# The last 128 columns of one matrix product turned round for three tiles of four, in a fused attention and MLP kernel

## The chip, the core and the metric

The kernel runs on one core of a Trainium2 chip. The metric is the device time of one execution in microseconds (us). Before the change the median of three executions is 261.24 us (261.08 to 261.54).

## What is computed

The input `x` has 2048 tokens of 640 values. Two branches read it and a gate mixes them. Of the reference, cut to what matters here:

```python
g = sigmoid((x * gate_w).sum(-1, keepdims=True))
a = linear_attention(x, wqkv, wo)                  # 32 heads of 20
h  = gelu(layernorm(x) @ w1)                       # 640 -> 640
hs = concat([h[:160] one token later, h[160:320] one earlier,
             h[320:480] two later,    h[480:] two earlier]) @ w2
x1 = x + hs
b  = x1 + gelu(layernorm(x1) @ w3) @ w4            # 640 -> 1728 -> 640
out = g * a + (1 - g) * b
```

The change is in the product with `w2` and in the sum `x1 = x + hs` behind it. The second layernorm needs, for each token, the sum and the sum of squares of `x1`.

## The kernel before

Tokens are cut into 16 tiles of 128 (t = 0 to 15) and 4 chunks of 512 (c = 0 to 3); 640 features are 5 slices of 128 (k = 0 to 4). The five engines each run a list of instructions in order, with semaphores between them. TensorE (PE) multiplies into PSUM, which has 8 banks of 512 fp32 columns; VectorE (DVE) and ScalarE (ACT) empty the banks; GpSimd (POOL) normalizes; SyncE (SP) issues nearly all DMAs, among them transposes by the crossbar (`dma_start_transpose`, L285).

The stages around the change:

- **W1** (`w1_group`, L1068): for chunk c and feature block j, 5 matmuls of 512 columns give h with features on partitions; ACT writes the gelu into `hsT` (L1074), shifted by one or two tokens. The block j = 4 takes four gelus, one for each group of 32 features.
- **W2** (`w2_tile`, L1076): for tile t the weights are slices of `hsT` and the moving operand is `w2`: 5 matmuls of 512 columns into one bank and 5 of 128 columns into the bank beside it (`pair()` takes two neighbouring banks). One DVE operation over 640 columns (`stt`, L1081, profile line L657) adds `x_tok` and stores the sum of each token in `st2[:, 0, t]`.
- **SQ** (`w2_sq`, L1083): ACT squares `x_tok` of tile t and stores the sum of squares (profile line L675).
- **S2** (`ln_chunk_stats`, L835): seven small POOL operations per chunk make mean and scale, once its four tiles have both sums.
- **N2 and T2** (`normalize` L853, `t_xn` L859): POOL writes the normalized tile into one of three `xn` buffers, and SP has it transposed into `xnT`.
- **W3** (`w3_group`, L1086): 13 groups of 5 matmuls of 512 columns per chunk read `xnT` of four tiles. `w3_half` (L1095) does the last 64 features of two chunks.
- **QN, QT, AT** (L1113 to L1158): the attention's quotients on DVE, their transposes on SP and its output products on PE.
- **W4** (L1202): the last product. For the first 128 output columns it already works turned: outputs on partitions, 512 tokens moving, then an ACT copy to `tlT`, a crossbar transpose to `tl` (`turn`, L1151) and sums on DVE.

**What sets the order.** Nothing is ordered by hand after the start. `_Items.run` (L352) is a planner in the program that builds the kernel. Every step is an item in a stream, with a duration, dependencies and lags. An item's priority is its duration plus the largest "lag plus priority" of what follows it (in its stream or by a dependency). The planner keeps its own model of when each engine is free. At each step it takes the item with the smallest `max(est, t_pe)`, where `t_pe` is when PE comes free and `est` is when the model has the item's inputs done plus 100 ns; then items of duration 0 (SQ, S2, N2, T2, QN); then the higher priority. Lags count in the priority, not in `est`. The order in which items are taken is the order of instructions on every engine, so an instruction that waits holds back all behind it on its engine. A PSUM bank is chosen in the same pass: `bank()` (L534) takes the one that the model has free first.

W1 and W2 are two streams that the planner interleaves by priority:

```python
IT.add("W1", ("w1", c, j), 1.08, ...)   # L1256
IT.add("W2", ("w2", t), 1.33, ...)      # L1264, needs w1(c, 4) and, for t % 4 == 3, w1(c + 1, 4)
IT.add("SQ", ("sq", t), 0.0, ...)       # L1265, needs w2(t)
```

The buffers `tlT` and `tl` lie in memory that `pk_tok`, the attention's keys, holds earlier (`ra` and `rb`, L473 and L474).

Of the kernel before, what the change touches and what calls it, by code (L numbers as in the profile page):

```python
# [6 lines left out]
F32 = mybir.dt.float32  # L7
ACTF = mybir.ActivationFunctionType
ALU = mybir.AluOpType

S = 2048
D = 640
# [3 lines left out]
NT = S // 128  # L16
NCH = S // 512
KD = D // 128
# [414 lines left out]
def _build(nc, A_x, A_wqkv, A_wo, B_w1, B_w2, B_w3, B_w4, gate_w, out, dbg=None, stop=None):  # L433
    sch = _Sched(nc)
# [37 lines left out]
    pa = Arena(SB_LO, SB_HI - SHARED)  # L472
# [3 lines left out]
    ps = nc.alloc_psum_tensor("ps", [128, 8, 512], F32)  # L476
# [9 lines left out]
    negh = pa.alloc("negh", [128, 4], F32)  # L486
    st1 = pa.alloc("st1", [128, 8, NT], F32)
    st2 = pa.alloc("st2", [128, 8, NT], F32)
    stg = pa.alloc("stg", [128, 4, NT], F32)
    lr = pa.alloc("lr", [128, NT, 2], F32)  # L490
    w3 = pa.alloc("w3", [128, KD, F], BF16)
    w1 = pa.alloc("w1", [128, KD, D], BF16)
    w2 = pa.alloc("w2", [128, KD, D], BF16)
    wo_aug = pa.alloc("wo_aug", [128, 6, D], BF16)
    x_tok = pa.alloc("x_tok", [128, NT, D], BF16)
    xnT = pa.alloc("xnT", [128, KD, S], BF16)
    hsT = pa.alloc("hsT", [128, KD, S + 4], BF16)
# [24 lines left out]
    tlT = rb.alloc("tlT", [128, 3, 512], BF16)  # L522
    tl = rb.alloc("tl", [128, 3, 4, 128], BF16)
# [10 lines left out]
    def bank():  # L534
        best = None
        for k_ in range(nbanks[0]):
            b = (bank_rr[0] + k_) % nbanks[0]
            if b in bank_pend or b in bank_hold:
                continue
            lk = sch.locks.get(b)  # L540
            tfree = 0.0 if lk is None else sch.ev_time.get((lk[1].sem, lk[1].val), 1e18)
            if best is None or tfree < best[0]:
                best = (tfree, b)
        bank_rr[0] = best[1] + 1
        bank_pend.add(best[1])
        return best[1]

    psf = ps[:, :, :].rearrange("p b n -> p (b n)")
    bank_hold = set()

    def pair():
        best = None
        for k_ in range(4):
            q_ = (bank_rr[0] // 2 + k_) % 4
            tf = 0.0
            ok = True
            for b in (2 * q_, 2 * q_ + 1):
                if b in bank_pend or b in bank_hold:
                    ok = False
                lk = sch.locks.get(b)  # L560
                if lk is not None:
                    tf = max(tf, sch.ev_time.get((lk[1].sem, lk[1].val), 1e18))
            if ok and (best is None or tf < best[0]):
                best = (tf, 2 * q_)
        b = best[1]
        bank_rr[0] = b + 2
        bank_pend.update((b, b + 1))
        return b
# [8 lines left out]
    def nfree(ap):  # L577
        n = 1
        for d_ in ap.shape[1:]:
            n *= d_  # L580
        return n

    def in_psum(ap):
        return ap.tensor.name == ps.name

    def act(fn, reads, writes, cost=None):
        if cost is None:
            n = nfree(writes[0])
            cost = max(150.0, 100.0 + 0.833 * n + (70.0 if (reads and in_psum(reads[0])) else 0.0))
            cost += 45.0 * max(0, len(reads) - 1)  # L590
        return sch.op("act", fn, reads, writes, cost=cost)

    def dve(fn, reads, writes, cost=None):
        if cost is None:
            n = nfree(writes[0])
            cost = 65.0 + n / 0.96
        return sch.op("dve", fn, reads, writes, cost=cost)
# [7 lines left out]
    def pe(fn, reads, writes, cost=500.0, after=None):  # L605
        for w_ in writes:
            sp_, rl = sch.rects(w_)
            if sp_ == "ps":
                for (_p0, _p1, lo, hi) in rl:
                    for b in range(lo // PS_BANK, (hi - 1) // PS_BANK + 1):  # L610
                        bank_pend.discard(b)
        return sch.op("pe", fn, reads, writes, cost=cost, after=after)

    def mm_group(out_ap, pairs, reads_extra=()):
        n = len(pairs)

        def fn(e, out_ap=out_ap, pairs=pairs, n=n):
            ins = None
            for i, (l, r) in enumerate(pairs):
                ins = e.matmul(out_ap, l, r, start=(i == 0), stop=(i == n - 1))  # L620
            return ins
        reads = [a for p in pairs for a in p] + list(reads_extra)
        return pe(fn, reads, [out_ap], cost=n * (max(nfree(pairs[0][1]), 24) * 0.4167 + 2.5))
# [28 lines left out]
    def stt(out_ap, in0, scalar, in1, op0, op1, accum=None):  # L652
        rd = [in0, in1] + ([scalar] if not isinstance(scalar, (int, float)) else [])
        n = nfree(out_ap)
        cost = (65.0 + n / 0.96) if (in_psum(in0) or in_psum(in1)) else (160.0 + 1.04 * n)
        if accum is not None:
            return dve(lambda e: e.scalar_tensor_tensor(out_ap, in0, scalar, in1, op0, op1, accum_out=accum), rd,  # L657
                       [out_ap, accum], cost=cost + 70.0)
        return dve(lambda e: e.scalar_tensor_tensor(out_ap, in0, scalar, in1, op0, op1), rd, [out_ap], cost=cost)  # L659
# [3 lines left out]
    def activation(out_ap, in_ap, func, scale=1.0, bias=0.0, accum=None):  # L663
        rd = [in_ap] + [a for a in (scale, bias) if not isinstance(a, (int, float))]
        wr = [out_ap] + ([accum] if accum is not None else [])
        n = nfree(out_ap)
        cost = max(150.0, 100.0 + 0.833 * n + (70.0 if in_psum(in_ap) else 0.0)) + 45.0 * (len(rd) - 1)
        if accum is not None:
            cost += 91.0
        st_ = ACT_SET.get(func)  # L670
        if st_ is not None and st_ != sch.act_func:
            cost += 1290.0
            sch.act_func = st_
        if accum is not None:
            return act(lambda e: e.activation(out_ap, in_ap, func, bias=bias, scale=scale, accum_out=accum), rd, wr, cost=cost)  # L675
        return act(lambda e: e.activation(out_ap, in_ap, func, bias=bias, scale=scale), rd, wr, cost=cost)  # L676
# [91 lines left out]
    IT = _Items()  # L768
# [66 lines left out]
    def ln_chunk_stats(st, c, rs):  # L835
        cs = slice(4 * c, 4 * c + 4)
        ts(pool, st[:, 2, cs], rs, 1.0 / D, 0.0, ALU.mult, ALU.add)
        ts(pool, st[:, 3, cs], st[:, 1, cs], 1.0 / D, EPS_LN, ALU.mult, ALU.add)
        tt(pool, st[:, 4, cs], st[:, 2, cs], st[:, 2, cs], ALU.mult)
        tt(pool, st[:, 5, cs], st[:, 3, cs], st[:, 4, cs], ALU.subtract)  # L840
        tt(pool, st[:, 6, cs], st[:, 5, cs], negh[:, 0:4], ALU.pow)
        tt(pool, st[:, 7, cs], st[:, 2, cs], st[:, 6, cs], ALU.mult)
        ts(pool, st[:, 7, cs], st[:, 7, cs], -1.0, 0.0, ALU.mult, ALU.add)
# [224 lines left out]
    def w1_group(c, j):  # L1068
# [3 lines left out]
        for (p0, p1, sh) in PIECES[j]:  # L1072
            o0 = 2 + 512 * c + sh
            activation(hsT[p0:p1, j, o0:o0 + 512], ps[p0:p1, b, :], ACTF.Gelu_apprx_tanh)  # L1074

    def w2_tile(t):  # L1076
        tok = slice(2 + 128 * t, 2 + 128 * (t + 1))
        b = pair()
        mm_group(ps[:, b, 0:512], [(hsT[:, k, tok], w2[:, k, 0:512]) for k in range(KD)])
        mm_group(ps[:, b + 1, 0:128], [(hsT[:, k, tok], w2[:, k, 512:D]) for k in range(KD)])  # L1080
        stt(x_tok[:, t, :], psf[:, 512 * b:512 * b + D], 1.0, x_tok[:, t, :], ALU.mult, ALU.add, accum=st2[:, 0, t:t + 1])  # L1081

    def w2_sq(t):  # L1083
        activation(junk[:, 0, :], x_tok[:, t, :], ACTF.Square, accum=st2[:, 1, t:t + 1])
# [163 lines left out]
    for c in range(NCH):  # L1248
        for j in range(KD):
            deps = [(("t1", u), 0.9) for u in range(4 * c, 4 * c + 4)] if j == 0 else []  # L1250
# [6 lines left out]
    for t in range(NT):  # L1257
        c = t // 4
        deps = [(("w1", c, KD - 1), GEL)]
        if t % 4 == 3 and c + 1 < NCH:  # L1260
            deps.append((("w1", c + 1, KD - 1), GEL))
        if t == 0:
            deps.append((("g", KD - 1), 0.0))
        IT.add("W2", ("w2", t), 1.33, lambda t=t: w2_tile(t), deps)  # L1264
        IT.add("SQ", ("sq", t), 0.0, lambda t=t: w2_sq(t), [(("w2", t), 1.0)])  # L1265
        if t % 4 == 3:
            IT.add("S2", ("s2", c), 0.0, lambda c=c: ln_chunk_stats(st2, c, st2[:, 0, 4 * c:4 * c + 4]), [(("sq", t), 1.0)])
    for u in range(NT):
        deps = [(("s2", u // 4), 3.2 + 0.9 * (u % 4))]
# [8 lines left out]
    for c in range(NCH):  # L1278
        for j in range(KFF):
            deps = []  # L1280
# [4 lines left out]
            if j == 0:  # L1285
                deps = deps0 + [(("t2", u), 0.9) for u in range(4 * c, 4 * c + 4)]
# [11 lines left out]
    for t in range(NT):  # L1298
        deps = [(("zb",), 1.0), (("q", max(t, 3)), 2.0)]
        if t < 7:  # L1300
            i = (5 * t) // 2 + 3
            deps.append((("w1", i // KD, i % KD), 0.0))
        else:
            i = 3 * (t - 7)
# [7 lines left out]
    for t in range(NT):  # L1312
        c = t // 4
        deps = [(("qt", t), 3.0), (("w4load",), 0.0), (("mq",), 1.0), (("mt",), 2.5)]
# [72 lines left out]
```

## Time and profile before

| | |
|---|---|
| median of three executions | 261.24 us |
| the profiled execution | 261.42 us |
| its span, first to last instruction | 259.7 us |
| PE busy | 255.9 us (99%) |
| DVE busy | 154.4 us (59%) |
| ACT busy | 111.6 us (43%) |
| POOL busy | 98.5 us (38%) |
| granted TensorE clock | 1.000 |

The profiled execution is 1.7 us longer than its span, which does not contain start and end of the program. Times in the trace count from the first instruction. PE stands for matmuls and PEld for the weight loads that run beside them. A matmul's listed duration (379 ns for 512 columns) is its latency; matmuls overlap, so what one costs is the distance from its start to the next one's start. In a timeline row the first number is the start, the second the time that the merged instructions took together, and brackets at the end hold the idle time before and what ended it. A line number in a row is often that of a helper: L620 is every matmul of `mm_group`, L676 every `activation` without a sum, L642 and L659 the DVE or POOL helpers `ts` and `stt`.

### The profile page before, as it was taken

How to read it: one execution, taken by the hardware profiler on the slowest of the kernel's cores; microseconds unless marked ns; L12 is line 12 of the kernel's file. 1: busy time of each engine (PE TensorE's matmuls, PEld its weight loads, DVE VectorE, ACT ScalarE, POOL GpSimd, SP SyncE). 2: the span in 40 equal slices, each digit the busy share in tenths (PEclk: the TensorE clock that was granted, in tenths of full speed). 3: DMA queues.
4: the chain of work that ended last, by engine and by line, in shares of the span. 5: the costliest groups of instructions: out<-in, count | busy, mean ns of one | idle time of the engine just before them, and what ended most of it. 6: DMA issues, size and time to landing. Idle time of an engine off the chain costs nothing.

```text
span 259.7 us, 3906 instructions
## 1 busy us (share of the span) xinstructions
PE 255.9 (99%) x1474; PEld 124.5 (48%) x1474; DVE 154.4 (59%) x286; ACT 111.6 (43%) x226; POOL 98.5 (38%) x154
## 2 busy tenths in 40 slices
PE   7999999999999999999999999999999999999996
PEld 3555555554445554555444444444444444444443
DVE  2497787889912799979995303998006510049136
ACT  1486767751355756694774240015510055200100
POOL 8103996869965018867663210111002210003000
PEclk9999999999999999999999999999999999999999
DMA  6868996551856993443796511115110030010222
GB/s 197 258 84 246 174 112 150 156 125 34 115 107 126 293 375 79 78 91 65 125 117 120 109 23 20 25 25 140 34 20 0 3 121 0 0 23 0 89 54 101
DMA packets 55668, 26.06 MB, mean 100 GB/s; under 512 B 46990, under 2 KB 54239, under 8 KB 55650
## 3 DMA queue, kind: packets, MB, share of 16 engines
q1 hardware_dynamic: 54146, 22.20, 39.1%
q0 software_dynamic: 1168, 3.28, 5.5%
q10 hardware_dynamic: 336, 0.35, 0.4%
q8 instruction: 11, 0.18, 0.3%
q14 instruction: 7, 0.06, 0.1%
HBM read 12.09 MB, written 2.67 MB: 57 GB/s over the span
## 4 chain that ended last, share of the span: by engine, by line
PE 97%; DMA 1%; DVE 0%; issue 0%
PE ps L620 61%; PE ps L1206 22%; PE ps L825 7%; PE ps L901 2%; PE ps L805 1%; DMA x_tok<-in_A_x_dram 1%; PE ps L1106 1%; PE ps L1184 1%; PE ps L631 1%; PE ps L902 1%; PE ps L979 0%; PE ps L1189 0%; PE ps L806 0%; PE ps L1012 0%; DVE xT L685 0%; DVE x_tok L659 0%
## 5 line engine op out<-in xcount | busy, mean ns | idle before, releaser
L620 PE MATMUL ps<-xnT,w 128*128 128x512 bf16 x360 | 81.5, 379 | 0.0
L620 PEld LDWEIGHTS ps<-xnT,w 128*128 128x128 bf16 x360 | 34.5, 98 | 39.3 <-issue 0.2
L659 DVE SCALAR_TENSOR_TENSOR x_tok<-ps,stg,abx 128x512 bf16<-128x512 f32 (+2 forms) x17 | 12.2, 717 | 60.3 <-PE ps L1206 60.2
L1206 PE MATMUL ps<-w,h2T 128*128 128x512 bf16 (+2 forms) x221 | 47.0, 366 | 0.0
L642 POOL TENSOR_SCALAR abx<-x_tok,stg 128x512 f32<-128x512 bf16 x16 | 12.4, 780 | 88.8 <-DVE x_tok L659 71.6
L642 POOL TENSOR_SCALAR xn<-x_tok,st 128x640 bf16<-128x640 bf16 x32 | 36.6, 1152 | 10.6 <-DMA xnT<-xn 10.1
L676 ACT ACTIVATE h2T<-ps 128x512 bf16<-128x512 f32 x52 | 29.9, 600 | 22.9 <-PE ps L620 22.9
L1206 PEld LDWEIGHTS ps<-w,h2T 128*128 128x128 bf16 x221 | 21.2, 98 | 24.1
L676 ACT ACTIVATE tlT<-ps 128x512 bf16<-128x512 f32 x8 | 4.8, 598 | 60.7 <-PE ps L620 49.6
L676 ACT ACTIVATE Er<-ps 128x640 bf16<-128x640 f32 x32 | 22.4, 707 | 18.3 <-PE ps L620 8.4
L675 ACT ACTIVATE junk<-x_tok 128x640 bf16<-128x640 bf16 x32 | 23.7, 740 | 5.3 <-DVE x_tok L657 4.9
L676 ACT ACTIVATE hsT<-ps 128x512 bf16<-128x512 f32 (+1 forms) x32 | 18.9, 595 | 14.4 <-PE ps L620 14.0
L620 PE MATMUL ps<-w,hsT 128*128 128x512 bf16 (+1 forms) x160 | 24.0, 299 | 0.0
L620 PE MATMUL ps<-wkg,xT 128*128 128x512 bf16 (+1 forms) x150 | 22.6, 299 | 0.0
L620 PE MATMUL ps<-M_sb,pqnT 128*128 128x512 bf16 x80 | 19.7, 379 | 0.0
L620 PEld LDWEIGHTS ps<-w,hsT 128*128 128x128 bf16 x160 | 13.4, 98 | 12.4
L620 PE MATMUL ps<-wq,xT 128*128 128x512 bf16 (+1 forms) x120 | 18.3, 299 | 0.0
L825 PE MATMUL ps<-pk_tok,x_tok 128*128 128x512 bf16 x80 | 17.8, 379 | 0.0
L657 DVE SCALAR_TENSOR_TENSOR x_tok<-ps,x_tok 128x640 bf16<-128x640 f32 x16 | 13.1, 821 | 7.6 <-PE ps L620 6.6
L659 DVE SCALAR_TENSOR_TENSOR abx<-ps,stg,abx 128x512 f32<-128x512 f32 x16 | 11.9, 748 | 8.9 <-PE ps L620 6.2
L642 DVE TENSOR_SCALAR Er<-Er 128x640 bf16<-128x640 bf16 x32 | 11.3, 354 | 9.0 <-ACT Er L676 8.5
L620 PEld LDWEIGHTS ps<-wkg,xT 128*128 128x128 bf16 x150 | 12.1, 98 | 9.0
(85 smaller groups left out, 286.4 us busy)
## 6 DMA issues: line engine op xcount, KB each, us to landing
w<-in_B_w_dram SPq DMA_DIRECT2D x1, 2160.0 KB, 9.1
w<-in_B_w_dram SPq DMA_DIRECT2D x1, 2080.0 KB, 14.6
x_tok<-in_A_x_dram SPq DMA_DIRECT2D x3, 640.0 KB, 5.7
out_dram<-x_tok SPq DMA_DIRECT2D x3, 640.0 KB, 3.4
w<-in_B_w_dram POOLq DMA_DIRECT2D x8, 160.0 KB, 4.4
wkg<-in_A_wqkv_dram SPq DMA_DIRECT2D x5, 160.0 KB, 4.7
wv<-in_A_wqkv_dram POOLq DMA_DIRECT2D x1, 800.0 KB, 6.1
x_tok<-in_A_x_dram SPq DMA_DIRECT2D x4, 160.0 KB, 3.2
```

The source lines that it names most:

```text
L620: ins = e.matmul(out_ap, l, r, start=(i == 0), stop=(i == n - 1))
L631: ins = e.transpose(o, s_, ident[:])
L642: return engf(lambda e: e.tensor_scalar(out_ap, in_ap, s1, s2, op0, op1), rd, [out_ap], cost=cost)
L657: return dve(lambda e: e.scalar_tensor_tensor(out_ap, in0, scalar, in1, op0, op1, accum_out=accum), rd, [out_ap, accum], cost=cost + 70.0)
L659: return dve(lambda e: e.scalar_tensor_tensor(out_ap, in0, scalar, in1, op0, op1), rd, [out_ap], cost=cost)
L675: return act(lambda e: e.activation(out_ap, in_ap, func, bias=bias, scale=scale, accum_out=accum), rd, wr, cost=cost)
L676: return act(lambda e: e.activation(out_ap, in_ap, func, bias=bias, scale=scale), rd, wr, cost=cost)
L805: e.matmul(ps[:, b, :], l, x_tok[:, t, 0:512], start=(t == 0), stop=(t == NT - 1))
L825: ins = e.matmul(ps[:, b, :], l, r, start=(t0 + q_ == 0), stop=(t0 + q_ == NT - 1))
L901: e.matmul(ps[:, b, 0:512], l, w[:, k, 0:512], start=(k == 0), stop=(k == KD - 1))
L902: return e.matmul(ps[:, b + 1, 0:n2], l, w[:, k, 512:512 + n2], start=(k == 0), stop=(k == KD - 1))
L1206: ins = e.matmul(o, l, r, start=False, stop=(i == KFF - 1), skip_group_check=shared)
```

## The change

For tiles t with t % 4 below 3, the last 128 output columns of W2 are no longer computed by 5 matmuls of 128 columns each. Once per chunk a new item `w2t` (`w2_turned`) computes them turned: the weights are `w2[:, k, 512:640]`, and 384 tokens of `hsT` move, 5 matmuls into one bank. ACT copies the result to `tlT`, and SP has it transposed into `tl`. The DVE operation of these tiles then covers 512 columns instead of 640, and a second new item `w2s` (`w2_turned_sum`) adds the turned part to `x_tok` for three tiles at once, sums it over its 128 columns and adds that to the sums in `st2`. Tile t % 4 == 3 is computed as before. The squares of all four tiles of a chunk now also wait for `w2s`.

```diff
+    st2t = pa.alloc("st2t", [128, NT], F32)
...
+    def w2_turned(c):
+        i = c % 2
+        b = bank()
+        mm_group(ps[:, b, 0:384], [(w2[:, k, 512:D], hsT[:, k, 2 + 512 * c:2 + 512 * c + 384]) for k in range(KD)])
+        activation(tlT[:, i, 0:384], ps[:, b, 0:384], ACTF.Copy)
+        sch.dma("sp", tl[:, i, 0:3, :], tlT[:, i, 0:384], "w2t%d" % i, transpose=True)
+
     def w2_tile(t):
         tok = slice(2 + 128 * t, 2 + 128 * (t + 1))
-        b = pair()
+        n = D if t % 4 == 3 else 512
+        b = pair() if n == D else bank()
         mm_group(ps[:, b, 0:512], [(hsT[:, k, tok], w2[:, k, 0:512]) for k in range(KD)])
-        mm_group(ps[:, b + 1, 0:128], [(hsT[:, k, tok], w2[:, k, 512:D]) for k in range(KD)])
-        stt(x_tok[:, t, :], psf[:, 512 * b:512 * b + D], 1.0, x_tok[:, t, :], ALU.mult, ALU.add, accum=st2[:, 0, t:t + 1])
+        if n == D:
+            mm_group(ps[:, b + 1, 0:128], [(hsT[:, k, tok], w2[:, k, 512:D]) for k in range(KD)])
+        stt(x_tok[:, t, 0:n], psf[:, 512 * b:512 * b + n], 1.0, x_tok[:, t, 0:n], ALU.mult, ALU.add, accum=st2[:, 0, t:t + 1])
+
+    def w2_turned_sum(c):
+        ts_ = slice(4 * c, 4 * c + 3)
+        xt = x_tok[:, ts_, 512:D]
+        dve(lambda e: e.tensor_tensor(xt, tl[:, c % 2, 0:3, :], xt, ALU.add), [tl[:, c % 2, 0:3, :], xt], [xt], cost=460.0)
+        dve(lambda e: e.tensor_reduce(st2t[:, ts_], xt, mybir.AxisListType.X, ALU.add), [xt], [st2t[:, ts_]], cost=460.0)
+        dve(lambda e: e.tensor_tensor(st2[:, 0, ts_], st2[:, 0, ts_], st2t[:, ts_], ALU.add), [st2[:, 0, ts_], st2t[:, ts_]], [st2[:, 0, ts_]], cost=100.0)
...
-        IT.add("W2", ("w2", t), 1.33, lambda t=t: w2_tile(t), deps)
-        IT.add("SQ", ("sq", t), 0.0, lambda t=t: w2_sq(t), [(("w2", t), 1.0)])
+        if t % 4 == 0:
+            IT.add("W2", ("w2t", c), 0.82, lambda c=c: w2_turned(c), list(deps))
+            IT.add("W2S", ("w2s", c), 0.0, lambda c=c: w2_turned_sum(c), [(("w2t", c), 4.0), (("w2", t + 2), 1.0)])
+        IT.add("W2", ("w2", t), 1.36 if t % 4 == 3 else 1.08, lambda t=t: w2_tile(t), deps)
+        IT.add("SQ", ("sq", t), 0.0, lambda t=t: w2_sq(t), [(("w2", t), 1.0), (("w2s", c), 1.0)])
```

## The prediction

> **What bounds the kernel now.** I read the page first, then the chain that ended last, then PE's timeline.
>
> ```profile
> span 259.7 us, 3906 instructions
> ...
> PE 255.9 (99%) x1474; PEld 124.5 (48%) x1474; DVE 154.4 (59%) x286; ACT 111.6 (43%) x226; POOL 98.5 (38%) x154
> ...
> PE 97%; DMA 1%; DVE 0%; issue 0%
> ```
>
> ```profile
> 102.54 1.24 PE L620 MATMUL ps<-xnT,w 128*128 128x512 bf16 x5
> 103.62 1.52 PE L620 MATMUL ps<-w,hsT 128*128 128x512 bf16 x10
> 104.98 1.24 PE L620 MATMUL ps<-xnT,w 128*128 128x512 bf16 x5
> 106.06 1.52 PE L620 MATMUL ps<-w,hsT 128*128 128x512 bf16 x10
> 107.42 1.24 PE L620 MATMUL ps<-xnT,w 128*128 128x512 bf16 x5
> 108.50 1.52 PE L620 MATMUL ps<-w,hsT 128*128 128x512 bf16 x10
> 109.86 2.32 PE L620 MATMUL ps<-xnT,w 128*128 128x512 bf16 x10
> 112.02 1.52 PE L620 MATMUL ps<-w,hsT 128*128 128x512 bf16 x10
> ```
>
> The last chain is 97% PE. In the timeline (start, time, ..., count) W1 groups (`xnT,w`) and W2 tiles (`w,hsT`) follow without a hole: 102.54 to 103.62 is 1.08 for five matmuls of 512 columns, 0.216 us each; 103.62 to 104.98 is 1.36 for five of 512 and five of 128, which leaves 0.28, so 0.056 us for one of 128. PE never waits in this stage, so the change can gain only by less work on PE, and loses whatever makes PE wait. Nothing later gives a wait back: PE is full to the end.
>
> **The change part by part.**
>
> *PE.* Twelve tiles lose five matmuls of 128 columns: 60 x 0.056 = 3.36 us. Four chunks gain five of 384. On the straight line through 0.056 (128) and 0.216 (512), one of 384 is 0.056 + 256 x 0.160/384 = 0.163; twenty are 3.25 us. The same columns move either way, 7680, and only the fixed 2 to 3 ns of 40 matmuls go: **0.1 us less**.
>
> *Weight loads.* Forty fewer.
>
> ```profile
> 81.69:119.35 37.66, 37.66 (x237) 19.61 (x236) 31.23 (x67) 25.11 (x52) 18.84 (x31) 1.00 0.60 170
> L620 PEld LDWEIGHTS ps<-w,hsT 128*128 128x128 bf16 x160 | 13.4, 98 | 12.4
> ```
>
> A load lists 98 ns, yet matmuls of 128 columns start every 56, so the loads lie under matmuls and I count them at nothing. If all 98 showed, the bound would be 40 x 0.098 = 3.9 us gained; the 56 speaks against it. The first row (window; time; busy us of PE, PEld, DVE, ACT, POOL; clock; DMA share; GB/s) says that in the W2 stage PE is full, DVE is at 31.23 of 37.66, and ACT at 25.11.
>
> The Trainium skill ("TensorE: Matmul & The Clock Gate", Back-to-back issue gap) gives about 81 ns per matmul of 128 columns and 131 ns for 512 where every matmul has its weight load. By that, with an estimated 114 ns for 384, the sum would be 60 x 81 - 20 x 114 = 2.6 us gained. The trace disagrees at both sizes (56 and 216), and the measurement decides.
>
> *DVE, ACT, SP: what is added.*
>
> ```profile
> L657 DVE SCALAR_TENSOR_TENSOR x_tok<-ps,x_tok 128x640 bf16<-128x640 f32 x16 | 13.1, 821 | 7.6 <-PE ps L620 6.6 <-ACT junk L675 0.6
> L659 DVE SCALAR_TENSOR_TENSOR abx<-ps,stg,abx 128x512 f32<-128x512 f32 x16 | 11.9, 748 | 8.9 <-PE ps L620 6.2 <-POOL abx L642 2.7
> L650 DVE TENSOR_TENSOR tlu<-tl,x_tok 128x512 f32<-128x512 bf16 x4 | 2.7, 682 | 0.0
> L1116 DVE TENSOR_REDUCE dnr<-qprod 128x32 f32<-128x640 f32 x16 | 13.1, 820 | 0.5
> L642 DVE TENSOR_SCALAR dnr<-dnr 128x32 f32<-128x32 f32 x16 | 4.1, 254 | 0.1
> L676 ACT ACTIVATE tlT<-ps 128x512 bf16<-128x512 f32 x8 | 4.8, 598 | 60.7 <-PE ps L620 49.6 <-PE ps L1206 11.1
> L675 ACT ACTIVATE junk<-x_tok 128x640 bf16<-128x640 bf16 x32 | 23.7, 740 | 5.3 <-DVE x_tok L657 4.9
> tl<-tlT SPq DMA_TRANSPOSE x8, 2.4
> L285 SPq DMA_TRANSPOSE tl<-tlT x8: 1189/1191/1829, 149.0 to 246.7; - x8
> ```
>
> DVE, per chunk: the add over 384 elements, 682 x 384/512 = 0.51 (bounds 0.25, the 32-element row, and 0.68); the reduce, 820 x 384/640 = 0.49 (0.25 to 0.82); the small add, 0.2 (up to 0.25). Together 1.2 us, 4.8 in all (3 to 7), less 12 x (0.821 - 0.748) = 0.9: **+3.9 us on DVE**, in a stage where 6.4 us are idle. ACT: four copies at 0.5 (0.6 at most). SP: four transposes, 1.2 us of issue and 2.4 to landing. None of this is on the path by itself: PE's own work covers it. It costs only where it makes PE late, and there are three places.
>
> *Which order.* The planner takes the higher priority. Worked by hand from durations and lags, against the last W2 tile: w1(3,3) 8.9, w2(8) 8.7, w1(3,4) 7.8, w2(9) 7.6, w2(10) 6.5; before, w1(3,4) stood above w2(10) and below w2(9). So two tiles instead of one follow w1(3,4), w2t(0) takes the place of w2(0) at 81.69, and w2t(2) runs just after w1(3,2). In trace times w1(3,4) then ends at 108.50 - 10 x 1.36 + 3 x 0.81 + 7 x 1.08 + 2 x 1.36 = 107.6, and after w2(9) and w2(10) PE is at 109.8, where before it was at 109.86. There, as before, w2(11) cannot start (the gelus of w1(3,4) are not done), and w3(0,0) and w3(0,1) fill in. They need the normalized chunk 0.
>
> *Place 1: the filler w3(0,0).*
>
> ```profile
> 99.72 3.69 POOL L642 TENSOR_SCALAR xn<-x_tok,st 128x640 bf16<-128x640 bf16 x3
> 101.67 1.74 POOL L642 TENSOR_SCALAR xn<-x_tok,st 128x640 bf16<-128x640 bf16 x2
> 104.40 1.98 POOL L642 TENSOR_SCALAR xn<-x_tok,st 128x640 bf16<-128x640 bf16 x1 [0.99 <-DMA xnT<-xn]
> 101.71 3.85 SPq L285 DMA_TRANSPOSE xnT<-xn  x3
> 106.41 1.39 SPq L285 DMA_TRANSPOSE xnT<-xn  x1
> DMA to landing us min/median/max: 2.6/2.6/4.3
> ```
>
> The fourth transpose of chunk 0 is issued at 106.41 and lands 2.6 later, at 109.0: only 0.85 us ahead of w3(0,0). Now w2t(2) runs at 103.6, its copy ends at about 105.0, and its transpose, taken before the fourth tile's, is queued between: third transpose to 105.9, w2t(2)'s to 107.2, the fourth issued at 107.2, landed at 109.8. The sums of chunk 0 end within 0.3 us of where they did: w2s(0) runs after w2(2) at about 90.3, and the squares follow on an ACT that has room. PE arrives at 109.8, so I count **0.2 us of wait** here, with 0 and 1.3 as ends: the POOL normalization takes 0.87 or 1.98 for the same tile, and one more or one less of the slow kind moves the landing by 1.1.
>
> The Trainium skill ("GPSIMD Engine Reference", Specifications) says that GpSimd shares its SBUF interfaces with VectorE and contends with instructions that read two SBUF inputs. The 0.87 and 1.98 agree in kind. The added add has two such inputs; by this rule each could stretch a normalization by about its own length, an estimated 0.5 us, which would leave the sum inside the ends above.
>
> *Place 2: the gelus of w1(3,4).*
>
> ```profile
> 108.70 2.44 ACT L676 ACTIVATE hsT<-ps 32x512 bf16<-32x512 f32 x4 [1.84 <-PE ps L620]
> 111.16 0.74 ACT L675 ACTIVATE junk<-x_tok 128x640 bf16<-128x640 bf16 x1
> ```
>
> Squares used to trickle; now four come together after w2s. With its read of the sum one takes 0.86 on ACT, four 3.4. DVE reaches w2s(1) at about 104.0 behind its queue of quotients and ends it at 105.2; four squares end at 109.5 (a gelu stands between), and the four gelus of w1(3,4) at 111.9 to 112.0, when PE wants w2(11) at 112.0. Before, they ended at 111.14. **0 to 0.2 us**; I take nothing beyond place 1.
>
> *Place 3: the transpose of w2t(1).* It is issued behind the big loads of w3 and w4.
>
> ```profile
> 84.56 8.24 SPq L289 DMA_DIRECT2D w<-in_B_w_dram  x4
> 96.00:98.00 2.00, 2.00 (x15) 1.06 (x13) 1.97 (x4) 1.71 (x6) 0.96 (x3) 1.00 1.08 364
> 98.00:100.00 2.00, 2.00 (x14) 0.95 (x12) 1.93 (x6) 1.93 (x4) 1.70 (x4) 1.00 0.23 63
> ```
>
> SP is in those four issues until 92.8, and the DMA engines are full until 98. w2t(0)'s transpose goes ahead of them and pushes both by 1.3; w2t(1)'s copy ends at 95, and its data lands by about 101. DVE wants it at 104: nothing, with 3 us of cover. If the cover were gone, DVE would stand still, then ACT at the squares behind, then PE at place 2.
>
> *Later squares.* Those of chunk 3 come some 8 us later than before, among the copies of the attention matrix:
>
> ```profile
> 124.95 0.74 ACT L675 ACTIVATE junk<-x_tok 128x640 bf16<-128x640 bf16 x1 [3.00 <-DVE x_tok L657]
> 129.03 2.67 ACT L676 ACTIVATE M_sb<-ps 128x512 bf16<-128x512 f32 x6
> 131.72 0.95 ACTq L289 DMA_DIRECT2D M_sb<-m_rows  x2
> 130.33 3.81 POOL L642 TENSOR_SCALAR xn<-x_tok,st 128x640 bf16<-128x640 bf16 x3
> 134.01 5.63 SPq L285 DMA_TRANSPOSE xnT<-xn  x4
> 149.36 2.35 PE L1106 MATMUL ps<-xnT,w 128*64 128x512 bf16 x20
> ```
>
> Copies, two issues and four squares are 2.67 + 0.95 + 3.44 = 7.1 us in which ACT empties no bank, while PE fills one per 1.08: six and a half of the eight. It fits, barely. The normalized chunk 3 comes later too. Its last square ended at 125.9, the first normalization began at 130.33 and the fourth transpose was issued by 139.6. With squares that end near 135, the same 4.5 us of statistics and about 8 us of normalizing and transposing, without the wait behind other transposes, it lands at about 147. Its first reader is the second half of the twenty matmuls from 149.36, at 150.5: 3 us of slack.
>
> *Sum.* -0.1 on PE, +0.2 at place 1: the profiled execution of 261.42 would become 261.5 (its span 259.8); on the median of 261.24, which is 0.18 lower, **261.3**.
>
> **The rivals.**
>
> *Slower, the filler comes late.* The mechanism is place 1 with a landing at 110.4 to 111.8. It decides from 109.8 on, and each us later is a us of PE, up to about 2, when w2(11) would have been ready anyway. For it: the landing that I work out has no margin left. Against: POOL, not SP, held the fourth tile before, and one fast normalization gives it back. 261.8 to 263.2, typically 262.2.
>
> *Slower, ACT in bunches.* The squares of place 2 start after 106, or the banks run out at 129 to 135. It decides when w2s(1) ends later than 105.4, or when ACT's 7.1 us become more than 8 x 1.08 = 8.6. Price 0.6 to 2 us: 261.8 to 263.2. For it: DVE has 31.23 busy of 37.66 and gets 3.9 more. Against: before, ACT lost 3.00 us at 124.95 and PE did not notice.
>
> *Faster, weight loads count.* If the 98 ns of the 40 loads showed after all, 261.24 - 3.9 = 257.3. The 56 ns between matmuls of 128 columns speak against it. By the figures of the skill's page quoted above it would be 258.6.
>
> *The turned part does not run where it should.* The copy into `tlT` must wait until the old contents are read. The last reader is the sum of the keys:
>
> ```profile
> 71.21 1.39 DVE L650 TENSOR_TENSOR zsum<-qprod,pk_tok 128x640 bf16<-128x640 f32 x1
> ```
>
> It ends at 72.6, ten us before w2t(0). No cost, and I give this no chance.
>
> **How the numbers follow.** Forecast (PE full, waits of 0 to 0.5 us): 0.60, own range 260.9 to 261.7. Filler late: 0.21. ACT in bunches: 0.14. Weight loads, or a gain that I don't see: 0.05. A measurement of this kernel tells about 0.2% (0.5 us) from no change, so same is 0.60, slower 0.21 + 0.14 = 0.35, faster 0.05. The range from 260.9 to 263.2 leaves out the faster case and the tail of the slower ones.
>
> **What would show it.** Right: the 384-column matmuls start 0.162 to 0.163 apart; PE busy stays at 99%; no wait of PE above 0.5 us between 80 and 150; the fourth transpose of chunk 0 lands at 109 to 110. Wrong: a hole in PE's timeline ahead of w3(0,0) or w2(11), or near 130, its waits naming a DMA of `xnT` or ACT; the transpose of w2t(1) landing after 104; or matmuls of 384 columns at less than 0.16.

## The result, and the profile after

The changed kernel takes **263.31 us** (median of five, 262.99 to 263.56), the kernel before on the same chip 261.24 (261.08 to 261.54): a ratio of 1.0068, with a 95% interval from 1.0049 to 1.0086 (the two medians alone give 1.0079). The change makes the kernel slower, by 1.8 us by the ratio and 2.07 by the medians. The profiled execution took 262.99 us.

From the page of the changed kernel come its span, the busy time of each engine, and the engines' shares of the chain that ended last:

```profile
span 261.1 us, 3826 instructions
...
PE 255.8 (98%) x1434; PEld 122.8 (47%) x1434; DVE 157.0 (60%) x298; ACT 114.2 (44%) x230; POOL 98.9 (38%) x154
...
PE 96%; ACT 1%; DMA 1%; issue 1%; DVE 0%
```

PE's busy time fell by 0.1 us, as the prediction has it, yet the span grew by 1.4. So PE stood still somewhere, and ACT has entered the chain. The waits of PE name one place that the kernel before lacks (total, times, longest), and PE's timeline shows where it is:

```profile
PE ps L621 <- ACT h2T L677: 1.5, 1, 1.5
```

```profile
119.11 8.80 PE L621 MATMUL ps<-xnT,w 128*128 128x512 bf16 x40
127.84 0.74 PE L1013 MATMUL ps<-wo_aug,Lt 64*64 64x512 bf16 x16
128.51 1.25 PE L621 MATMUL ps<-xnT,w 128*128 128x512 bf16 x5
131.30 6.00 PE L621 MATMUL ps<-xnT,w 128*128 128x512 bf16 x27 [1.54 <-ACT h2T L677]
```

The forty matmuls are the eight W3 groups w3(0,2) to w3(0,9). The sixteen belong to `m_quads`, which makes the attention matrix; the next five are w3(0,10), and the last row begins with w3(0,11). A group of five takes 1.08 us, so w3(0,11) should have started at 129.59. It started at 131.30, 1.71 later.

The rest of the account fits. Before the change, PE's timeline has w3(0,2), the first of the forty, here:

```profile
119.35 8.80 PE L620 MATMUL ps<-xnT,w 128*128 128x512 bf16 x40
```

It came at 119.35 and now comes at 119.11, 0.24 earlier. The chain gives where PE reaches the stage of W1 and W2, before and after (start, time, what):

```profile
78.51 49.63 PE ps L620 x291
```

```profile
78.37 48.48 PE ps L621 x246
```

That is 0.14 earlier; the other 0.10 is the shorter work in between, as predicted. 1.71 less 0.24 is 1.47, and the span grew by 1.4. The profiled executions differ by 1.57, the medians by 2.07. No trace shows the half microsecond between: one execution of each was profiled, that of the changed kernel being the shortest of its five.

What PE waited for stands in the timeline of ACT:

```profile
124.20 3.26 ACT L677 ACTIVATE h2T<-ps 128x512 bf16<-128x512 f32 x6
127.36 0.73 ACT L676 ACTIVATE junk<-x_tok 128x640 bf16<-128x640 bf16 x1
128.21 0.74 ACT L676 ACTIVATE junk<-x_tok 128x640 bf16<-128x640 bf16 x1
129.07 0.74 ACT L676 ACTIVATE junk<-x_tok 128x640 bf16<-128x640 bf16 x1
129.94 0.74 ACT L676 ACTIVATE junk<-x_tok 128x640 bf16<-128x640 bf16 x1
130.67 0.58 ACT L677 ACTIVATE h2T<-ps 128x512 bf16<-128x512 f32 x1
131.15 2.60 ACT L677 ACTIVATE M_sb<-ps 128x512 bf16<-128x512 f32 x6
133.78 0.80 ACTq L289 DMA_DIRECT2D M_sb<-m_rows  x2
```

The four squares of chunk 3 (`junk<-x_tok`) stand in a row ahead of the gelu of w3(0,9) and ahead of the six copies that empty `m_quads`. `m_quads` takes six of the eight PSUM banks at once. Its copies come after the squares, so from 127.8 on PE has two banks left. w3(0,9) and w3(0,10) fill them, and w3(0,11) must have the bank of w3(0,9) back. That bank's gelu starts at 130.67, when the fourth square is done. The chain that ended last, between 126 and 136 us (start, time, what), walks over just these instructions (`junk` x2 is a square and the read of its sum):

```profile
127.36 0.83 ACT junk L676 x2
...
128.21 0.84 ACT junk L676 x2
...
130.77 0.49 ACT h2T L677
131.26 0.05 issue
131.30 4.71 PE ps L621 x21
```

Before, the chain passed this place on PE alone, because the last square of chunk 3 had ended at 125.9 and the copies stood directly behind the gelus.

The three places that the prediction names, in the trace of the changed kernel. First the fourth normalization of chunk 0, the two transposes behind it, and w3(0,0):

```profile
103.44 0.88 POOL L643 TENSOR_SCALAR xn<-x_tok,st 128x640 bf16<-128x640 bf16 x1 [0.36 <-DMA xnT<-xn]
...
104.96 1.18 SPq L285 DMA_TRANSPOSE tl<-tlT  x1
106.18 1.28 SPq L285 DMA_TRANSPOSE xnT<-xn  x1
...
109.64 1.24 PE L621 MATMUL ps<-xnT,w 128*128 128x512 bf16 x5
```

Then the gelus of w1(3,4), the first square behind them, and the sum `w2s(1)` for which the squares waited:

```profile
107.17 0.35 DVE L1096 TENSOR_TENSOR x_tok<-tl,x_tok 128x384 bf16<-128x384 bf16 x1
...
107.68 2.44 ACT L677 ACTIVATE hsT<-ps 32x512 bf16<-32x512 f32 x4 [1.56 <-PE ps L621]
110.14 0.74 ACT L676 ACTIVATE junk<-x_tok 128x640 bf16<-128x640 bf16 x1
```

And the transpose of `w2t(1)` behind the loads of w3 and w4, with its time to landing:

```profile
94.78 1.72 SPq L285 DMA_TRANSPOSE tl<-tlT  x1
...
DMA to landing us min/median/max: 8.2/8.2/8.2
```

None of them makes PE wait. The groups of the added work (busy time, mean ns | idle before them):

```profile
L621 PE MATMUL ps<-hsT,w 128*128 128x384 bf16 x20 | 3.9, 325 | 0.0
L677 ACT ACTIVATE tlT<-ps 128x384 bf16<-128x384 f32 x4 | 1.9, 488 | 0.4 <-PE ps L621 0.4
L1096 DVE TENSOR_TENSOR x_tok<-tl,x_tok 128x384 bf16<-128x384 bf16 x4 | 1.8, 448 | 0.1
L1097 DVE TENSOR_REDUCE st2t<-x_tok 128x3 f32<-128x384 bf16 x4 | 2.2, 553 | 0.1
L1098 DVE TENSOR_TENSOR st<-st,st2t 128x3 f32<-128x3 f32 x4 | 0.6, 162 | 0.1
```

### The profile page after: what moved, and what is told of

Read it like the earlier page. It is cut to its first block, busy times and chain, and to the rows that moved or that the text cites. A ratio compares the mean times of both kernels' runs of the same rounds, so it can differ in the third digit from the quotient of the medians.

```text
span 261.1 us, 3826 instructions
## 1 busy us (share of the span) xinstructions
PE 255.8 (98%) x1434; PEld 122.8 (47%) x1434; DVE 157.0 (60%) x298; ACT 114.2 (44%) x230; POOL 98.9 (38%) x154
## 4 chain that ended last, share of the span: by engine, by line
PE 96%; ACT 1%; DMA 1%; issue 1%; DVE 0%
PE ps L621 60%; PE ps L1223 22%; PE ps L826 7%; PE ps L902 2%; PE ps L806 1%; DMA x_tok<-in_A_x_dram 1%; ACT junk L676 1%; PE ps L1123 1%; PE ps L1201 1%; PE ps L903 1%; PE ps L632 1%; PE ps L980 0%; PE ps L1206 0%; PE ps L807 0%; ACT h2T L677 0%
## 5 line engine op out<-in xcount | busy, mean ns | idle before, releaser
L643 POOL TENSOR_SCALAR abx<-x_tok,stg 128x512 f32<-128x512 bf16 x16 | 13.0, 814 | 84.3 <-DVE x_tok L660 65.4
L643 POOL TENSOR_SCALAR xn<-x_tok,st 128x640 bf16<-128x640 bf16 x32 | 34.9, 1099 | 8.2 <-DMA xnT<-xn 7.8
L677 ACT ACTIVATE tlT<-ps 128x512 bf16<-128x512 f32 (+1 forms) x12 | 6.7, 561 | 61.2 <-PE ps L621 50.1
L621 PE MATMUL ps<-w,hsT 128*128 128x512 bf16 (+1 forms) x100 | 20.7, 347 | 0.0
L643 POOL TENSOR_SCALAR st<-st 128x4 f32<-128x4 f32 x20 | 6.3, 316 | 26.8 <-DVE dnr L643 12.1
L1150 DVE TENSOR_TENSOR pq_tok<-pq_tok,dnr 128x600 bf16<-128x600 bf16 (+1 forms) x32 | 14.9, 507 | 0.6
```

The costliest lines, as they stand in the source:

```text
L643: return engf(lambda e: e.tensor_scalar(out_ap, in_ap, s1, s2, op0, op1), rd, [out_ap], cost=cost)
L1150: dve(lambda e, o=o, i0=i0, i1=i1: e.tensor_tensor(o, i0, i1, ALU.mult), [i0, dnr[:, 1, sd, :]], [o], cost=cost)
```

## The experiments

**Theory A**: the 2 us are the wait of w3(0,11), made by the order of ACT: the four squares of a chunk, which now start together after `w2s`, stand ahead of a gelu and of the copies that free six banks. **Theory B**: they are the added work itself (DVE 2.6 us more, ACT 2.6 us more, four more transposes), wherever it stands.

The first four kernels ran on one chip, beside the kernel before at 261.43 us (median of 35). The first takes the wait of the squares away and leaves the added sums, copies and transposes in place. It leaves out the squares of the last 128 columns of the twelve turned tiles, so its squares are also shorter (0.63 us instead of 0.74).

```diff
 def w2_sq(t):
-    activation(junk[:, 0, :], x_tok[:, t, :], ACTF.Square, accum=st2[:, 1, t:t + 1])
+    n = D if t % 4 == 3 else 512
+    activation(junk[:, 0, 0:n], x_tok[:, t, 0:n], ACTF.Square, accum=st2[:, 1, t:t + 1])
...
-    IT.add("SQ", ("sq", t), 0.0, ..., [(("w2", t), 1.0), (("w2s", c), 1.0)])
+    IT.add("SQ", ("sq", t), 0.0, ..., [(("w2", t), 1.0)])
```

> The turned product stays as in the changed kernel, but the squares of the twelve turned tiles cover only the first 512 columns and so no longer wait for w2s; the squares of the last 128 columns of these tiles are left out. Theory A (banks: the four squares of chunk 3 come as a bunch just ahead of the gelu that frees the bank of w3(0,11), while six of the eight banks wait for the copies of m_quads behind the same squares): the 1.9 us step at w3(0,11) falls back to 0.22, PE is full again, time 261.0 to 261.4, ratio to before 0.999 to 1.001. Theory B (the added work itself, 3.9 us on VectorE and four more transposes on SP, makes PE late): all of that work is still there, so the time stays at 262.5 to 263.5.

Measured: 261.85 us (261.50 to 262.74), ratio 1.0014 (0.9999 to 1.0028), 0.4 above the range of A and far below that of B. In ACT's timeline the copies now stand directly behind the gelus, and no hole at w3(0,11) is left:

```profile
127.17 2.62 ACT L677 ACTIVATE M_sb<-ps 128x512 bf16<-128x512 f32 x6
```

About 1.6 of the 2 us are gone with the wait, while the added sums, copies and transposes are all still there. That is A's side, and B falls as the main cause; since the squares are shorter here, the next run is the cleaner test. What is left, 0.4 us, has about the size of two small waits of PE in its profile, less the 0.1 gained; that they are the cause is argued from the sizes alone:

```profile
PE ps L621 <- DMA pqnT<-pq_tok: 0.4, 1, 0.4
...
PE ps L621 <- ACT h2T L677: 0.2, 1, 0.2
```

The second keeps the whole change and only makes `m_quads` depend on a W3 group two earlier; the planner then takes it one group earlier, ahead of the squares:

```diff
-    IT.add("KVF", ("mq",), 0.0, m_quads, deps=[(("w3", 0, 7), 0.0)])
+    IT.add("KVF", ("mq",), 0.0, m_quads, deps=[(("w3", 0, 5), 0.0)])
```

> The changed kernel with one number changed: m_quads depends on w3(0,5) instead of w3(0,7), so that its six copies go ahead of the four squares of chunk 3 on ScalarE instead of behind them. The same instructions on every engine, squares just as late and just as bunched. Theory A (banks): the six banks come free ahead of the squares, w3(0,11) finds one, no step of PE above 0.4 us between 80 and 149 us, time 261.0 to 261.5. Theory B (added work on VectorE and SP): nothing of it is taken away, 262.5 to 263.5. A third possibility, that ScalarE is simply overloaded there (7 us without a gelu): the wait only moves to a later w3 group, 262 to 263.5.

Measured: 261.63 us (261.28 to 261.96), ratio 1.0006 (0.9991 to 1.0021), 0.1 above A's range. Its ACT timeline and PE timeline:

```profile
127.16 2.62 ACT L677 ACTIVATE M_sb<-ps 128x512 bf16<-128x512 f32 x6
129.81 0.86 ACTq L289 DMA_DIRECT2D M_sb<-m_rows  x2
130.72 0.74 ACT L676 ACTIVATE junk<-x_tok 128x640 bf16<-128x640 bf16 x1 [0.94 <-DVE pq_tok L1150]
...
134.04 4.97 ACT L677 ACTIVATE h2T<-ps 128x512 bf16<-128x512 f32 x10
```

```profile
127.46 11.82 PE L621 MATMUL ps<-xnT,w 128*128 128x512 bf16 x53 [0.16 <-ACT h2T L677]
```

The same instructions in another order: ACT takes no gelu from 127.16 to 134.04, 6.9 us, and PE runs 53 matmuls with no hole but 0.16 us ahead of them, because the copies free the six banks first. So a bunch of this length costs nothing by itself; it costs by standing in front of the copies.

The third and fourth do the change for some chunks only:

```diff
-    n = D if t % 4 == 3 else 512
+    n = D if t % 4 == 3 or not ((t // 4) < 3) else 512      # the third kernel
+    n = D if t % 4 == 3 or not ((t // 4) == 3) else 512     # the fourth
...
-    if t % 4 == 0:
+    if t % 4 == 0 and c < 3:       # the fourth: c == 3; the W2 times and the squares' dependency likewise
```

> Chunks 0 to 2 turned, chunk 3 as in the kernel before. Theory A, strictly (the bunch of chunk 3 is what costs): no bunch of four squares ahead of the copies, PE full or nearly so, 261.0 to 261.8. Theory A, wider (any delay of the squares into the time of m_quads costs; those of chunk 2 are late as well): a part of the wait stays, 0.3 to 1.2 us, 261.5 to 262.5. Theory B (added work): three quarters of the loss, 262.6 to 262.9.

Measured: 262.76 us (262.38 to 263.13), ratio 1.0047 (1.0032 to 1.0061). The time lies in B's range and above both of A's, so by the time alone this run speaks for B; the second run, with all of the added work at 261.63, speaks against it, and so does the trace. A in its narrow form, that chunk 3's squares alone cost, is wrong: with chunk 3 as before, 1.3 us are lost elsewhere. PE's timeline has two waits, 1.0 us together, and ACT's shows what stands ahead of each release:

```profile
114.34 1.53 PE L621 MATMUL ps<-w,hsT 128*128 128x512 bf16 x10 [0.63 <-ACT h2T L677]
...
124.88 1.47 PE L621 MATMUL ps<-xnT,w 128*128 128x512 bf16 x6 [0.35 <-ACT M_sb L677]
```

```profile
112.83 0.74 ACT L676 ACTIVATE junk<-x_tok 128x640 bf16<-128x640 bf16 x1
113.69 0.60 ACT L677 ACTIVATE h2T<-ps 128x512 bf16<-128x512 f32 x1
...
123.41 0.74 ACT L676 ACTIVATE junk<-x_tok 128x640 bf16<-128x640 bf16 x1
124.14 0.68 ACT L677 ACTIVATE M_sb<-ps 128x640 bf16<-128x640 f32 x1
```

The first is the gelu of w3(0,0) behind the four squares of chunk 1, the second the copy of another part of the attention matrix behind six squares. It is the same mechanism with other squares; 0.3 of the 1.3 us stay without a wait that names them. In the changed kernel the four squares of chunk 1 stand ahead of the same gelu (110.14 to 113.59) and PE does not wait. There the tiles of chunk 3 that follow take one bank each, and in the third kernel two; that this is the difference is argued from the code and was not tried by itself.

> Only chunk 3 turned, chunks 0 to 2 as in the kernel before. Theory A, strictly (the squares of chunk 3 wait for w2s and come as a bunch): if the bunch alone is enough, the full loss, 262.8 to 263.4; but with less ahead of it on ScalarE, w3(0,7) is done earlier and the copies may be taken ahead of the squares, as in the run with the copies first, and then 261.0 to 261.5, with the squares at 128 us or later and no wait of PE. Theory B (added work): a quarter of the loss, 261.7 to 261.9.

Measured: 261.54 us (261.12 to 261.61), ratio 0.9998 (0.9984 to 1.0012), at the upper end of what A expects with the copies first. The planner here put the copies ahead of the squares by itself (copies at 127.67, squares from 131.42), and no wait was left. So turning chunk 3 costs nothing when its squares stand behind the copies, and the run can't say what it costs when they don't.

The last four ran on another chip, beside the kernel before at 261.42 us (median of 17). The fifth makes the order alone, in the kernel before, with nothing turned:

```diff
-    IT.add("KVF", ("mq",), 0.0, m_quads, deps=[(("w3", 0, 7), 0.0)])
+    IT.add("KVF", ("mq",), 0.0, m_quads, deps=[(("w3", 0, 9), None), (("sq", NT - 1), None)])
...
-    IT.add("SQ", ("sq", t), 0.0, ..., [(("w2", t), 1.0)])
+    IT.add("SQ", ("sq", t), 0.0, ..., [(("w2", t), 1.0)] + ([(("w3", 0, 7), 0.0)] if t == 12 else []))
```

> The kernel before, nothing turned, only two dependencies changed: the squares of chunk 3 wait for w3(0,7), and m_quads comes behind them and behind w3(0,9), so that ScalarE has the order of the changed kernel: four squares, the gelu of w3(0,9), six copies. Theory A (banks behind a bunch of squares): the wait appears without any turned work, a step of 1.6 to 2.1 us at w3(0,11), time 262.7 to 263.4. Theory B (the added work on VectorE and SP makes PE late): none of it is here, 261.1 to 261.7.

Measured: 263.24 us (262.97 to 263.35), ratio 1.0071 (1.0058 to 1.0084), and in PE's timeline:

```profile
131.38 9.88 PE L620 MATMUL ps<-xnT,w 128*128 128x512 bf16 x45 [1.60 <-ACT h2T L676]
```

The kernel before, with only its squares and copies ordered like that, shows the same hole at the same group and the same time as the changed kernel (1.0068). The order is enough for the loss; the turned product isn't needed for it.

The sixth and seventh are the changed kernel with three and with two of the four squares ahead of the copies:

```diff
-    IT.add("SQ", ("sq", t), 0.0, ..., [(("w2", t), 1.0), (("w2s", c), 1.0)])
+    IT.add("SQ", ("sq", t), 0.0, ..., [(("w2", t), 1.0), (("w2s", c), 1.0)] + ([(("mq",), None)] if t == 15 else []))   # seventh: t == 14
```

> The changed kernel, but the square of tile 15 waits until m_quads is taken: three squares instead of four stand ahead of the gelu of w3(0,9). Theory A: the wait shrinks by one square, 0.86 us of ScalarE, from 1.7 to 0.8 to 0.9; time 0.9 less than the changed kernel's 263.31, 262.2 to 262.7. Theory B: no change, 263.0 to 263.6.

> The same with two squares behind m_quads and two ahead. Theory A: 1.7 less 2 x 0.86, no wait or up to 0.2 at w3(0,11); 261.3 to 261.8. Theory B: 263.0 to 263.6.

Measured: 262.46 us (262.33 to 262.62), ratio 1.0041 (1.0029 to 1.0053) for three, and 261.95 (261.59 to 263.75), ratio 1.0029 (1.0015 to 1.0043) for two squares ahead. PE's timeline, the sixth kernel and then the seventh:

```profile
130.71 9.89 PE L621 MATMUL ps<-xnT,w 128*128 128x512 bf16 x44 [0.68 <-ACT h2T L677]
```

```profile
128.32 10.96 PE L621 MATMUL ps<-xnT,w 128*128 128x512 bf16 x49
```

Four squares ahead give a wait of 1.54 us, three 0.68 (a little under the 0.8 to 0.9 expected), two none. The step is 0.86, the distance of one square to the next on ACT (128.21 to 129.07), and 0.68 less 0.86 is below nothing. The seventh's time is above the 261.3 to 261.8 expected. Its profiled execution took 261.59 and shows only a new wait of 0.3 us, at `w3_half` for the normalized chunk 3; the executions up to 263.75 were not profiled, and what they lost stays open.

The eighth turns the other knob: the four squares stay ahead of the gelu, but `m_quads` depends on a W3 group three later; the planner then takes it five groups later:

```diff
-    IT.add("KVF", ("mq",), 0.0, m_quads, deps=[(("w3", 0, 7), 0.0)])
+    IT.add("KVF", ("mq",), 0.0, m_quads, deps=[(("w3", 0, 10), 0.0)])
```

> The changed kernel with m_quads depending on w3(0,10) instead of w3(0,7): the four squares stay ahead of the gelu of w3(0,9), but the six banks are not yet taken. Theory A in its narrow form (it takes both, the bunch and the six taken banks): no wait at w3(0,11). The copies then come 5 us later and may make the attention's first product a(0) wait, up to 1.2 us there: 261.3 to 262.7. If the bunch alone were enough, 1.7 us would stay at w3(0,11) and the time at 263 or more.

Measured: 262.75 us (262.75 to 263.13), ratio 1.0057 (1.0045 to 1.0069), just above the expected 261.3 to 262.7. PE's timeline:

```profile
119.32 14.19 PE L621 MATMUL ps<-xnT,w 128*128 128x512 bf16 x64
...
140.70 1.24 PE L621 MATMUL ps<-M_sb,pqnT 128*128 128x512 bf16 x5 [1.01 <-DMA M_sb<-m_rows]
```

With all eight banks to turn over, PE runs 64 matmuls past the four squares without a stop. The wait at w3(0,11) therefore needs both, the bunch and the six taken banks. The late copies then make another wait, of the first attention product for the loaded part of `M_sb`, so this kernel gains only a little.

No version beats the kernel before. The first, second and fourth can't be told from it (their intervals hold 1), and the most that there was to win is the 0.1 us of PE.

## Why the prediction was wrong, point by point

The forecast of 261.3 was wrong, and the case that came true is the rival "ACT in bunches" in its second form, "the banks run out at 129 to 135", to which I gave 0.14 together with its first form. Its price of 0.6 to 2 us holds the wait of 1.5 to 1.7. The measured 263.31 lies far above the forecast's own range, 260.9 to 261.7, and 0.1 above the end of the whole range (by the ratio, 261.24 x 1.0068 = 263.0, just inside it).

*The step that failed* is "Later squares". It counts copies, issues and squares as 7.1 us without an emptied bank against eight banks of 1.08 us and says: "It fits, barely." Two things are wrong in it. It sets PE's store at eight banks, although the copies that it counts are those of six banks that `m_quads` holds until they are done. And it takes the order copies, then squares, from the trace of before. In that order the sum is right: the second experiment has 6.9 us without a gelu and no hole. The planner took the other order, squares first. Probably `w2s(3)` was done in its model before it came to `m_quads`; in the trace it ended at 125.6 and `m_quads` began at 127.84, but what the model had is not known. In that order PE has two banks, 2.2 us, against four squares of 0.86 = 3.4 us. The point from which the rival decides, "more than 8 x 1.08 = 8.6", should have been about 1.9 us of squares ahead of the copies (3.4 less the wait of 1.5); the runs with two squares (1.7, no wait) and three (2.6, a wait of 0.7) lie on either side of it.

I worked the order out by hand for the place around w2(10), and did not do it for this one, where the squares and `m_quads` came due close together.

*PE's gain*: right. The matmuls of 384 columns start 0.161 to 0.166 us apart, 0.163 on average, and the work came out 0.10 us less.

By the estimate made from the figures of the Trainium skill ("TensorE: Matmul & The Clock Gate", Back-to-back issue gap) the same stage would have been 2.6 us shorter; the trace again disagrees.

*Weight loads*: right. Forty fewer loads, and nothing but the 0.1 us.

*The added work*: DVE grew by 157.0 - 154.4 = 2.6 us instead of 3.9. The three added operations took 1.8 + 2.2 + 0.6 = 4.6 us, close to the 4.8 of the sum: the add is shorter than counted (0.35 us in three of four cases instead of 0.51), the reduce longer (0.55 instead of 0.49). The mis-sized term is the saving on the operation that empties the bank. Over 512 columns it takes 0.686 us, not the 0.748 read from another operation, so twelve of them save 1.6 us instead of 0.9:

```profile
L658 DVE SCALAR_TENSOR_TENSOR x_tok<-ps,x_tok 128x512 bf16<-128x512 f32 x12 | 8.2, 686 | 5.9 <-PE ps L621 5.7
```

4.6 less 1.6 is 3.0; the 0.4 between this and 2.6 is not placed. By itself the added work costs little, as predicted: the second experiment carries it all at 261.63.

*Order*: w1(3,4), w2(9) and w2(10) ran as worked out, and PE came to w3(0,0) at 109.64 (predicted 109.8). One filler was enough instead of two: w2(11) followed at 110.72.

*Place 1*: the wait of 0.2 did not come, nor did it follow from the figures given, which have the landing and PE both at 109.8. The fourth normalization took 0.88 us instead of 1.98 and began earlier. Its transpose was issued at 106.18, not 107.2. It landed 2.7 us later, at 108.9.

*Place 2*: no wait, but for another reason than the one given. `w2s(1)` ran at 107.17, not at 104.0, and the planner put the gelus of w1(3,4) ahead of the squares. I had named 105.4 as the point from which a late sum costs; that would hold only for squares that stand ahead of the gelus.

*Place 3*: right in its outcome. The transpose landed 8.2 us after 94.78, at 103.0 instead of 101, still 4.2 ahead of `w2s(1)` at 107.17.

*The normalized chunk 3*: the landing "at about 147" was forecast 3 us too early. In the changed kernel its fourth transpose was issued at 147.4 and landed 2.6 later, at 150.0; PE came to its first reader at 151.9, but only because it was itself 1.5 late. In the second and seventh experiments, where the wait at w3(0,11) is gone, none of the "3 us of slack" is left: the twenty matmuls of `w3_half` take 2.65 us in the second instead of 2.35, and in the seventh PE waits 0.3 there.

*The chances*: 0.60 for "same" rested on three places worked out and on a fourth, the banks, of which I had written that it barely fits.

## What to carry to other kernels

Here one engine was full, and 2.6 us of added work on each of two neighbours was nearly free (0.2 us in the second experiment). What cost was where an instruction came to stand in an in-order queue, and what its successors held at that time. Before counting how long an engine may stay away from emptying banks, count the banks that are already promised to someone who stands behind the same work: here six of eight. And where a change makes a trickle of instructions wait for one event, work out the order around each place where the bunch can land, for it will land somewhere (in the changed kernel at one place, in the third at two others).

## What the runs showed of the hardware that I had not expected

A crossbar transpose issued directly behind large loads in the same queue landed after 8.2 us; those of `tlT` before the change took 2.4. The row above shows it once, in the changed kernel.

The POOL normalization of one tile took 0.88 us in the changed kernel and 1.98 before, on the same data, a microsecond apart in the schedule. In the kernel before, a DVE multiply with two operands in SBUF ran inside it, at 104.97:

```profile
104.97 0.82 DVE L650 TENSOR_TENSOR qprod<-pq_tok,zb 128x640 f32<-128x640 bf16 x1
```

In the changed kernel the normalization (103.44 to 104.32) was over before DVE began its next multiply of that kind. The rest of the two traces shows the same. Before the change, the twelve normalizations with a `qprod` or `zsum` multiply beside them took 1.1 to 2.1 us, the twenty others 0.87 to 0.89. In the changed kernel, the one add of `w2s` that took 0.73 us instead of 0.35 (at 118.39) began while POOL normalized (118.04 to 118.92). This is a coincidence in time, seen many times; no run varies it by itself.

It fits what the Trainium skill ("GPSIMD Engine Reference", Specifications) says of SBUF interfaces shared with VectorE.
